# Relu's first weight as a second scalar operand, and a bias tile's load moved behind a store

## The chip, the cores and the metric

The kernel runs on one core of one Trainium2 chip. The metric is the device time of one execution in microseconds (us). Engines are named as in the profile: PE (matrix multiply), ACT (ScalarE), DVE (VectorE), POOL (GpSimd), and SP, whose queue issues almost all DMAs.

## The reference

Attention over 2 batches, 8 heads, 576 positions and head size 64, with a learned position bias, then a mixture of 4 experts over 1152 tokens, then a gated block in the same width of 512. What the change touches is the bias:

```python
psi_rel = np.log1p(np.abs(rel))                       # distance |i - j|
psi_i = np.log1p(np.maximum(pos[:, None], 1.0))
x = (psi_rel / psi_i)[..., None]
h = np.maximum(x @ w1 + b1, 0.0)                      # 32 hidden units
bias = h @ w2                                         # 8 heads
scores = scores + bias.transpose(2, 0, 1)[None]       # before the softmax
```

Since psi_i is positive, h is computed as max(w1 * log1p(distance) + b1 * psi_i, 0) / psi_i, and the division comes after the product with w2.

## The kernel before, in words

**Order of the work.** The kernel hands every operation to a planner (`Plan`) with an estimated time per engine, a priority, the buffers that it reads and writes, and operations that it comes `after`. The planner plays the work through in its own time and fixes one static order of instructions for each engine and for SP's queue. On the chip each engine keeps to its order and waits, by semaphores, for data and for buffers alone. An `after` shapes the order; it is no wait on the chip. All estimates stay as they are in what the change does not touch.

**The bias.** One DMA brings a table `cs` (line 337): the distances' logarithms (`tab`, 576 columns, the same in all 128 partitions), `neg_` (psi of the rows), `rinv` (1/psi), `cw` (w1 and b1, one column each) and `w2s`. Partitions are four groups of 32 hidden units. The bias rows come in 36 units `u` of 16 rows, each of four groups `g` (four rows each). `bias_group` makes a unit as follows. Each of four buffers `hh` takes one Relu over `n` columns (n is 576 for the first unit, 464 for the eighth, falls to 304 in the middle and rises again): three on DVE (line 376) and one on ACT (line 378), or all four on DVE in odd units among the first eight. DVE computes max(t, -b1 psi), which is the Relu less b1 psi; what is missing there is added later as a constant column `corr`, one of which (`corr[1]`) is zero for the group that ACT did. PE multiplies with `w2s` into PSUM (`pb`, line 390). The "side" copy (`put`, line 408 on ACT or 410 on DVE) scales by `rinv`, adds `corr` and writes a staging buffer `bst`; a "mirror" copy (line 239) fills the other side; a DMA stores the unit in DRAM, in `bias_d` (line 421). There are eight `hh` buffers and at first five `bst`.

**Who reads it.** Bias tiles `bt` of 128 rows are loaded from `bias_d` with shifted rows. The first tile, for the first eight units, is loaded in two halves of 64 rows (line 487): the first half needs units 0 to 3, the second units 4 to 7. The first attention groups then need `bt` in DVE's reduction (line 516), and all their later steps come behind it. Later tiles are loaded whole (line 476). The first 8 units have the highest rank (`bias0`), the next 8 `bias1`, the other 20 `bias2`; the latter are spread among the attention work until about 120 us. Expert matmuls (lines 772, 785), which PE uses to fill its time, start when the first attention groups are done, near 70 us.

**Ahead of the first Relu** stand, in the kernel before, a scaling of `tab` by w1 on ACT (line 345) and three scalings on DVE (`scales`, lines 340 to 342). `corr_mm` (line 353) and `corr_copy` (lines 357 and 359) make the constant column from b1 and w2.

Of the kernel before, what the change touches and what calls it, by code (L numbers as in the profile page):

```python
# [9 lines left out]
F32 = mybir.dt.float32  # L10
U32 = mybir.dt.uint32
F32R = mybir.dt.float32r
AF = mybir.ActivationFunctionType
ALU = mybir.AluOpType
# [3 lines left out]
B, H, S, D = 2, 8, 576, 64  # L18
HID = 32
P = 128  # L20
# [21 lines left out]
ENGINES = {"kcast": "ACT DVE", "ksub": "POOL DVE", "qcast": "DVE", "qsub": "DVE", "pt": "ACT DVE", "tail": "ACT DVE", "side": "ACT DVE", "mirror": "POOL ACT", "mirror0": "ACT DVE",  # L42
           "whi": "ACT DVE", "wlo": "DVE", "xhi": "DVE", "xlo": "POOL DVE", "rb": "ACT DVE", "rx": "ACT DVE", "s64": "DVE",
           "wsum": "POOL DVE", "whi2": "ACT", "wlo2": "DVE", "px": "ACT DVE", "xsum": "DVE", "xhi2": "ACT", "xlo2": "DVE", "hmul": "DVE", "hlo": "DVE"}
# [49 lines left out]
class Plan:  # L94
# [9 lines left out]
    def op(self, eng, fn, r=(), w=(), rw=(), hold=(), prio=0, lock=False, after=(), size=0, late=0):  # L104

        o = Op()
        o.eng, o.fn, o.prio, o.lock, o.size = eng, fn, prio, lock, size
        o.after, o.n, o.done, o.late = [], len(self.ops), False, late
        deps = set(after)
        for b in r:  # L110
            deps.update(b.writers)
        for b in rw:
            deps.update(b.writers)
            deps.update(b.readers)
        for b in rw:
            b.writers, b.readers = [o], []
        for b in w:
            b.writers.append(o)
        for b in r:
            b.readers.append(o)  # L120
        deps.discard(o)
        o.left = len(deps)
        for d in deps:
            d.after.append(o)
        o.bufs = list({id(b): b for b in (*r, *w, *rw, *hold)}.values())
        for b in o.bufs:
            b.left += 1
        self.ops.append(o)
        return o
# [102 lines left out]
def tile_kernel(ctx, tc, qd, kd, kf, vd, cst, probs, w1r, w2r, war, wbr, wor, out):  # L232
    nc = tc.nc
    plan = Plan()
    op = plan.op
# [14 lines left out]
    def t_psum(n, engs="ACT DVE"):  # L250
        est = {"ACT": n / 1.2 + 55, "DVE": n / 0.96 + 68}
        return {e: est[e] for e in engs.split()}
# [32 lines left out]
    hp = tp(hp_stack, "hp", side="right")  # L285
# [50 lines left out]
    rinv, cw, w2s = cs_t[:, S + NG:S + NG + NU], cs_t[:, S + NG + NU:S + NG + NU + 2], cs_t[:, S + NG + NU + 2:]  # L336
    op({"SP": 440}, lambda e: nc.sync.dma_start(out=cs_t, in_=cst), w=[cs], size=P * 3160)

    def scales(e):
        nc.vector.tensor_scalar(out=pos, in0=neg_.rearrange("p (u g) -> p u g", g=4)[:, :, 4 - pos.shape[2]:], scalar1=cw[:, 1:2], scalar2=None, op0=ALU.mult)  # L340
        nc.vector.tensor_scalar(out=neg_, in0=neg_, scalar1=cw[:, 1:2], scalar2=-1.0, op0=ALU.mult, op1=ALU.mult)
        nc.vector.tensor_scalar(out=w2s, in0=w2s, scalar1=8.0, scalar2=None, op0=ALU.mult)

    lg = Buf(t=cs_t)
    op({"ACT": S / 1.2 + 200}, lambda e: nc.scalar.activation(out=tab, in_=tab, func=AF.Copy, scale=cw[:, 0:1]), r=[cs], w=[lg], prio=-1)
    op({"DVE": 450}, scales, r=[cs], w=[lg])
    cs = lg
    pc, cr = new("tv", "pc"), Buf(t=cs_t)


    def corr_mm(e):
        for g in range(4):
            nc.tensor.matmul(pc.t[32 * g:32 * g + 32, 0:1], w2s, cw[:, 1:2], start=True, stop=True)

    def corr_copy(e):
        for n, x in corr.items():
            nc.vector.tensor_copy(x, pc.t[:, 0:1])
            for g in range(4 - n, 4):
                nc.vector.memset(x[32 * g:32 * g + 32], 0.0)

    def dist(u):
        before, after = 16 * u + 15, S - 16 * u
        return before, after, max(before + 1, after)

    rows, early = [], []

    def bias_group(u, rank):
        pri, acts = RANK[rank], RELUS[rank] if u % 2 == 0 or rank != "bias0" else 0
        before, after, n = dist(u)
        hs = []  # L370
        for g in range(4):
            G = 4 * u + g
            hh = new("hh")
            hs.append(hh)
            if g < 4 - acts:
                op({"DVE": n / 1.92 + 130}, lambda e, hh=hh, G=G: nc.vector.tensor_scalar(out=hh.t[:, :n], in0=tab[:, :n], scalar1=neg_[:, G:G + 1], scalar2=None, op0=ALU.max), r=[cs], w=[hh], prio=pri, lock=True)  # L376
            else:
                op({"ACT": n / 1.2 + 220}, lambda e, hh=hh, G=G: nc.scalar.activation(out=hh.t[:, :n], in_=tab[:, :n], func=AF.Relu, bias=pos[:, u, g - 4:][:, :1]), r=[cs], w=[hh], prio=pri)
        pb = new("tv" if n <= 512 else "s", "pb")
        bst = new("bst")  # L380


        def base():
            return (pb.t, 0) if n <= 512 else (pb.t.rearrange("p a b -> p (a b)"), 512 - n // 2)

        def mm(e):
            t, o = base()
            for lo, hi in ((0, n),) if n <= 512 else ((0, n // 2), (n // 2, n)):
                for g in range(4):
                    nc.tensor.matmul(t[32 * g:32 * g + 32, o + lo:o + hi], w2s, hs[g].t[:, lo:hi], start=True, stop=True)  # L390

        op({"PE": n * 1.67 + 170}, mm, r=[*hs, cs], w=[pb], hold=[bst], prio=pri)


        def ends():
            t, o = base()
            b = bst.t
            if before >= after:
                side = b[:, 0:before + 1], t[:, o:o + 1 + before][:, ::-1]
                rest = b[:, before + 1:before + after], b[:, before - after + 1:before][:, ::-1]  # L400
            else:
                side = b[:, before:before + after], t[:, o:o + after]
                rest = b[:, 0:before], b[:, before + 1:2 * before + 1][:, ::-1]
            return side, rest

        def put(e, out, src):
            if e == "ACT":
                nc.scalar.activation(out=out, in_=src, func=AF.Identity, scale=rinv[:, u:u + 1], bias=corr[acts])  # L408
            else:
                nc.vector.tensor_scalar(out=out, in0=src, scalar1=rinv[:, u:u + 1], scalar2=corr[acts], op0=ALU.mult, op1=ALU.add)  # L410

        def mirror(e):
            copy(e, *ends()[1])

        m = min(before, after - 1)
        side = op({e: v + 95 for e, v in t_psum(n, ENGINES["side"]).items()}, lambda e: put(e, *ends()[0]), r=[pb, cr], w=[bst], prio=pri)
        op({e: v for e, v in {"POOL": 2 * m + 150, "ACT": m / 1.2 + 95, "DVE": m / 0.96 + 68}.items() if e in ENGINES["mirror0" if rank == "bias0" else "mirror"].split()}, mirror, w=[bst], after=[side], prio=pri)
        rows.append(Buf(t=bias_d))

        def store(e):  # L420
            nc.sync.dma_start(out=bias_d[16 * u:16 * u + 16, :, S - before:S + after].rearrange("i h j -> (i h) j"), in_=bst.t[:, :before + after])

        o = op({"SP": 440}, store, r=[bst], w=[rows[u]], prio=pri, size=P * 4 * (before + after))
        if u == P // 16 - 1:
            early.append(o)

# [7 lines left out]
    def bias_rows(i0, n, h, nh):  # L436
        row = H * BW - 1
        o = i0 * H * BW + h * BW + S - i0
        x = bias_d.rearrange("i h j -> (i h j)")[o:o + n * row].rearrange("(i w) -> i w", w=row)
        return x[:, :nh * BW].rearrange("i (h j) -> i h j", h=nh)[:, :, :S]  # L440
# [25 lines left out]
    def bias_tile(m, t):  # L466
        for x in bias_seq[-3:]:
            if x[:2] == (m, t):
                return x[2]
        bt = new("bt")  # L470
        bias_seq.append((m, t, bt))

        def load(e):
            b = bt.t
            if t < 4:
                nc.sync.dma_start(out=b, in_=bias_rows(t * P, P, 2 * m, 2))
            else:
                nc.sync.dma_start(out=b[0:D, 0:1], in_=bias_rows(4 * P, D, 2 * m, 1))
                rest = bias_rows(4 * P, D, 2 * m + 1, 1)
                nc.sync.dma_start(out=b[D:P, 0:1, :S - D], in_=rest[:, :, D:])  # L480
                nc.sync.dma_start(out=b[D:P, 0:1, S - D:], in_=rest[:, :, :D])

        need = min(P * t + P, S) // 16
        if t == m == 0:
            for h in range(2):
                r = slice(D * h, D * h + D)
                op({"SP": 440}, lambda e, h=h, r=r: nc.sync.dma_start(out=bt.t[r], in_=bias_rows(D * h, D, 0, 2)), r=rows[4 * h:4 * h + 4], w=[bt], size=D * 8 * S)
        else:
            op({"SP": 440 if t < 4 else 1320}, load, r=rows[:need], w=[bt], size=P * 8 * S, late=1000 if t else 0)
        return bt  # L490
# [642 lines left out]
    for b in range(B):  # L1133
        QK[0, b, 0] = plain(0, b)
    op({"PE": 600}, corr_mm, r=[cs], w=[pc])
    op({"DVE": 400}, corr_copy, r=[pc], w=[cr])
    for u in range(NU):
        bias_group(u, "bias0" if u < P // 16 else "bias1" if u < 256 // 16 else "bias2")
    for g in groups:
# [225 lines left out]
```

## Time and profile before

| | |
|---|---|
| median of 3 runs | 791.68 us (790.96 to 793.36) |
| the profiled execution | 791.38 us |
| its span, first to last instruction | 789.6 us |
| PE busy in the span | 774.2 us (98%) |
| DVE busy in the span | 649.5 us (82%) |
| ACT busy in the span | 404.3 us (51%) |

Times of instructions are from the start of the span. A busy PE is an engine with a matmul under way, not one at its peak. Most executions of one program agree within 0.3%.

### The profile page before, as it was taken

The page shows a single profiled execution, that of the slowest core. Times are in us where ns is not written, and L with a number is a line of the kernel's source. Part 1 is how long each engine was busy: PE and PEld are TensorE (multiplying, and loading weights), DVE is VectorE, ACT ScalarE, POOL GpSimd, SP SyncE. Part 2 cuts the span into 40 slices and gives each one's busy share as a digit, 9 for nine tenths or more (in the row PEclk, how much of TensorE's full clock was granted, in tenths as well). Part 3 has the DMA queues.
Part 4 walks back from the last instruction along what each step waited for, and adds up shares of the span by engine and source line. Part 5 has one row for each costly group of instructions (what it writes and reads, how often), then busy time and mean ns, then how long its engine had stood idle before and what let it go on. Part 6 is the DMA issues. An engine that isn't in the chain of part 4 may idle for free.

```text
span 789.6 us, 13146 instructions
## 1 busy us (share of the span) xinstructions
PE 774.2 (98%) x4933; PEld 662.3 (84%) x4933; DVE 649.5 (82%) x1374; ACT 404.3 (51%) x848; POOL 28.1 (4%) x46
## 2 busy tenths in 40 slices
PE   7998999999999999999999999999999999999997
PEld 3475678888988888888888888889889999999996
DVE  7899986889896687998989998988698985757545
ACT  6877765677766543544544535344466532433321
POOL 0000100000000000000000000010010100000000
PEclk9999999999999999999999999999999999999999
DMA  6996658677563134455545653545405340301103
GB/s 233 327 344 215 232 178 276 218 243 244 179 208 98 45 96 127 134 166 175 160 126 159 204 175 120 166 132 161 134 1 183 112 160 1 107 27 55 54 1 120
DMA packets 46432, 120.31 MB, mean 152 GB/s; under 512 B 5024, under 2 KB 9376, under 8 KB 46368
## 3 DMA queue, kind: packets, MB, share of 16 engines
q1 hardware_dynamic: 46224, 119.34, 46.6%
q8 instruction: 39, 0.64, 0.3%
q14 instruction: 25, 0.20, 0.1%
q10 hardware_dynamic: 144, 0.13, 0.0%
HBM read 93.62 MB, written 25.84 MB: 151 GB/s over the span
## 4 chain that ended last, share of the span: by engine, by line
PE 90%; DVE 6%; ACT 1%; issue 1%; DMA 1%; DVEq 0%; ACTq 0%
PE pz L785 32%; PE up L883 14%; PE pw L1030 9%; PE up L772 8%; PE pb L390 4%; PE pv L613 4%; PE pr L1030 4%; PE ps L513 4%; PE pt L548 4%; PE pq L1030 2%; PE ps L531 1%; PE pz L1110 1%; DVE pr L516 1%; DVE k L453 1%; PE rp L593 1%
## 5 line engine op out<-in xcount | busy, mean ns | idle before, releaser
L785 PE MATMUL pz<-wh,hh 128*128 128x512 f32 x386 | 153.2, 397 | 0.0
L785 PE MATMUL pz<-wh,hl 128*128 128x512 f32 x386 | 151.3, 392 | 0.0
L785 PE MATMUL pz<-wl,hh 128*128 128x512 f32 x386 | 151.2, 392 | 0.0
L785 PEld LDWEIGHTS pz<-wl,hh 128*128 128x128 f32 x386 | 72.5, 188 | 15.9
L785 PEld LDWEIGHTS pz<-wh,hh 128*128 128x128 f32 x386 | 72.5, 188 | 14.2 <-issue 1.8
L785 PEld LDWEIGHTS pz<-wh,hl 128*128 128x128 f32 x386 | 72.5, 188 | 12.2
L239 ACT COPY ct<-pw 128x640 f32<-128x640 f32 (+3 forms) x48 | 27.9, 582 | 85.0 <-PE pw L1030 85.0
L516 DVE CUSTOM_DVE_ANT_0 pr<-ps,bt 128x576 f32<-128x576 f32 (+1 forms) x80 | 59.9, 753 | 13.9 <-PE ps L513 11.3
L658 DVE TENSOR_TENSOR wl<-wst,wh 128x1024 fp32r<-128x1024 f32 (+1 forms) x60 | 69.7, 1162 | 1.9 <-ACT wh L239 1.6
L526 ACT ACTIVATE pr<-pr,sums 128x576 f32<-128x576 f32 x72 | 56.1, 780 | 15.3 <-DVE sums L516 10.4
L772 PE MATMUL up<-x_h,wh 128*128 128x256 f32 (+1 forms) x200 | 61.7, 308 | 0.7 <-DVE hl L796 0.7
L239 ACT CAST wh<-wst 128x1024 fp32r<-128x1024 f32 (+1 forms) x56 | 54.5, 974 | 15.1 <-PE pz L785 7.8
L772 PE MATMUL up<-x_h,wl 128*128 128x256 f32 (+1 forms) x200 | 57.3, 286 | 0.0
L772 PE MATMUL up<-x_l,wh 128*128 128x256 f32 (+1 forms) x200 | 57.2, 286 | 0.0
L239 ACT COPY ptb<-pt 128x512 f32<-128x512 f32 (+3 forms) x98 | 40.3, 438 | 30.8 <-PE pt L548 25.4
L376 DVE TENSOR_SCALAR hh<-cs 128x560 f32<-128x560 f32 (+17 forms) x112 | 43.9, 448 | 3.8 <-PE pb L390 3.6
L239 ACT COPY ct<-up 128x448 f32<-128x448 f32 x39 | 20.7, 531 | 47.8 <-PE up L883 47.6
L613 PE MATMUL pv<-ptb,v 128*64 128x128 f32 (+2 forms) x480 | 44.1, 331 | 0.3 <-ACT bst L408 0.3
L883 PE MATMUL up<-xb,wsh 128*128 128x448 f32 x156 | 44.3, 365 | 0.0
L1125 DVE TENSOR_TENSOR acc<-pz,acc 128x512 f32<-128x512 f32 x44 | 30.2, 689 | 15.9 <-PE pz L785 14.9
L772 PEld LDWEIGHTS up<-x_h,wh 128*128 128x128 f32 x200 | 37.6, 188 | 6.5 <-issue 3.0
L548 PE MATMUL pt<-ident,pr 128*128 128x128 f32 x288 | 41.7, 275 | 0.0
(194 smaller groups left out, 1844.8 us busy)
## 6 DMA issues: line engine op xcount, KB each, us to landing
wst<-in_w1r SPq DMA_DIRECT2D x30, 512.0 KB, 4.4
wst<-in_w2r SPq DMA_DIRECT2D x30, 512.0 KB, 4.5
bias_d<-bst SPq DMA_DIRECT2D x36, 295.5 KB, 4.1
bt<-bias_d SPq DMA_DIRECT2D x15, 576.0 KB, 5.3
v<-in_vd SPq DMA_DIRECT2D x24, 320.0 KB, 4.3
s<-in_war SPq DMA_DIRECT2D x12, 512.0 KB, 4.9
wz_d<-hl SPq DMA_DIRECT2D x24, 256.0 KB, 2.5
s<-in_wbr SPq DMA_DIRECT2D x12, 512.0 KB, 4.9
```

The costliest lines, as they stand in the source:

```text
L239: (nc.scalar.copy if e == "ACT" else engine[e].tensor_copy)(out, in_)
L376: op({"DVE": n / 1.92 + 130}, lambda e, hh=hh, G=G: nc.vector.tensor_scalar(out=hh.t[:, :n], in0=tab[:, :n], scalar1=neg_[:, G:G + 1], sca ...
L390: nc.tensor.matmul(t[32 * g:32 * g + 32, o + lo:o + hi], w2s, hs[g].t[:, lo:hi], start=True, stop=True)
L516: nc.vector.tensor_tensor_reduce(out=pr.t[r0:r1, c].rearrange("p (a b) -> p a b", a=2), in0=ps.t[r0:r1, :, :HS], in1=bt.t[r0:r1, c].rearra ...
L526: nc.scalar.activation(out=pr.t[:, c], in_=pr.t[:, c], func=AF.Exp, scale=-1.0, bias=sums.t[:, neg:neg + 1], accum_out=sums.t[:, col:col + 1])
L548: nc.tensor.transpose(pt.t[:, kt * P:kt * P + P], pr.t[:, s, k0:k0 + P], ident)
L613: nc.tensor.matmul(pv.t[s * D:(s + 1) * D, :w], V.t[:, s, kt * D:(kt + 1) * D], ptb.t[:, blk, :w], start=(kt == 0), stop=(kt == 4))
L658: op(t_two(1024 - skip, ENGINES["wlo"]), lambda e: engine[e].tensor_tensor(out=w.t[1][:, skip:], in0=wst.t[:, skip:], in1=f(w.t[0][:, skip ...
L772: nc.tensor.matmul(u.t[:, :n], block(a, ft, d), x_at(x, d, lo, n), start=(d == 0 and j == 0), stop=(d == 3 and j == 2))
L785: nc.tensor.matmul(z.t, a[:, ft, tt * P:(tt + 1) * P], bb[:, ft, :], start=(first and ft == 0 and j == 0), stop=(final and ft == 1 and j = ...
L883: nc.tensor.matmul(bank.t[:, :n], s(a, k), x(b, k), start=(first and k == 0 and i == 0), stop=(stop and k == 1 and i == 2), skip_group_che ...
L1030: nc.tensor.matmul(o_, s[:, k], d[:, k], start=(first and k == 0 and i == 0), stop=(k == 1 and i == 2), skip_group_check=True)
```

## The change

The table `tab` is no longer scaled ahead of the Relus. DVE's Relu takes two operations with two scalars of one value per partition: it multiplies by w1 and takes the maximum with -b1 psi. ACT's Relu takes w1 as its `scale` operand, beside the `bias` operand that it had. Of the scalings, -b1 psi is made on DVE into a buffer of its own, b1 psi for ACT's groups on ACT, and the factor 8 goes from `w2s` to `rinv` (on DVE, with a lower rank) and to the constant column. POOL sets the `corr` columns to zero in advance, and `corr_copy` is two instructions in place of two copies and a memset. `corr_mm` needs only the table's DMA. The two half loads of the first bias tile come `after` the store of the seventh unit (u = 6) in the planner.

```diff
--- before.py
+++ after.py
@@ -336,15 +336,11 @@
     rinv, cw, w2s = cs_t[:, S + NG:S + NG + NU], cs_t[:, S + NG + NU:S + NG + NU + 2], cs_t[:, S + NG + NU + 2:]
     op({"SP": 440}, lambda e: nc.sync.dma_start(out=cs_t, in_=cst), w=[cs], size=P * 3160)
 
-    def scales(e):
-        nc.vector.tensor_scalar(out=pos, in0=neg_.rearrange("p (u g) -> p u g", g=4)[:, :, 4 - pos.shape[2]:], scalar1=cw[:, 1:2], scalar2=None, op0=ALU.mult)
-        nc.vector.tensor_scalar(out=neg_, in0=neg_, scalar1=cw[:, 1:2], scalar2=-1.0, op0=ALU.mult, op1=ALU.mult)
-        nc.vector.tensor_scalar(out=w2s, in0=w2s, scalar1=8.0, scalar2=None, op0=ALU.mult)
-
-    lg = Buf(t=cs_t)
-    op({"ACT": S / 1.2 + 200}, lambda e: nc.scalar.activation(out=tab, in_=tab, func=AF.Copy, scale=cw[:, 0:1]), r=[cs], w=[lg], prio=-1)
-    op({"DVE": 450}, scales, r=[cs], w=[lg])
-    cs = lg
+    psi, neg_ = neg_, hp.tile([P, NG], F32, name="neg")
+    NEG, POS, RI = Buf(t=neg_), Buf(t=pos), Buf(t=cs_t)
+    op({"DVE": 220}, lambda e: nc.vector.tensor_scalar(out=neg_, in0=psi, scalar1=cw[:, 1:2], scalar2=-1.0, op0=ALU.mult, op1=ALU.mult), r=[cs], w=[NEG], prio=-1)
+    op({"ACT": 220}, lambda e: nc.scalar.activation(out=pos, in_=psi.rearrange("p (u g) -> p u g", g=4)[:, :, 4 - pos.shape[2]:], func=AF.Copy, scale=cw[:, 1:2]), r=[cs], w=[POS], prio=-1)
+    op({"DVE": 90}, lambda e: nc.vector.tensor_scalar(out=rinv, in0=rinv, scalar1=8.0, scalar2=None, op0=ALU.mult), r=[cs], w=[RI], after=[], prio=0.1)
     pc, cr = new("tv", "pc"), Buf(t=cs_t)
 
 
@@ -352,17 +348,18 @@
         for g in range(4):
             nc.tensor.matmul(pc.t[32 * g:32 * g + 32, 0:1], w2s, cw[:, 1:2], start=True, stop=True)
 
+    for n, x in corr.items():
+        nc.gpsimd.memset(x, 0.0)
+
     def corr_copy(e):
         for n, x in corr.items():
-            nc.vector.tensor_copy(x, pc.t[:, 0:1])
-            for g in range(4 - n, 4):
-                nc.vector.memset(x[32 * g:32 * g + 32], 0.0)
+            nc.vector.tensor_scalar(out=x[:P - 32 * n], in0=pc.t[:P - 32 * n, 0:1], scalar1=8.0, scalar2=None, op0=ALU.mult)
 
     def dist(u):
         before, after = 16 * u + 15, S - 16 * u
         return before, after, max(before + 1, after)
 
-    rows, early = [], []
+    rows, early, sixth = [], [], []
 
     def bias_group(u, rank):
         pri, acts = RANK[rank], RELUS[rank] if u % 2 == 0 or rank != "bias0" else 0
@@ -373,9 +370,9 @@
             hh = new("hh")
             hs.append(hh)
             if g < 4 - acts:
-                op({"DVE": n / 1.92 + 130}, lambda e, hh=hh, G=G: nc.vector.tensor_scalar(out=hh.t[:, :n], in0=tab[:, :n], scalar1=neg_[:, G:G + 1], scalar2=None, op0=ALU.max), r=[cs], w=[hh], prio=pri, lock=True)
+                op({"DVE": n / 1.92 + 130}, lambda e, hh=hh, G=G: nc.vector.tensor_scalar(out=hh.t[:, :n], in0=tab[:, :n], scalar1=cw[:, 0:1], scalar2=neg_[:, G:G + 1], op0=ALU.mult, op1=ALU.max), r=[cs, NEG], w=[hh], prio=pri, lock=True)
             else:
-                op({"ACT": n / 1.2 + 220}, lambda e, hh=hh, G=G: nc.scalar.activation(out=hh.t[:, :n], in_=tab[:, :n], func=AF.Relu, bias=pos[:, u, g - 4:][:, :1]), r=[cs], w=[hh], prio=pri)
+                op({"ACT": n / 1.2 + 220}, lambda e, hh=hh, G=G: nc.scalar.activation(out=hh.t[:, :n], in_=tab[:, :n], func=AF.Relu, scale=cw[:, 0:1], bias=pos[:, u, g - 4:][:, :1]), r=[cs, POS], w=[hh], prio=pri)
         pb = new("tv" if n <= 512 else "s", "pb")
         bst = new("bst")
 
@@ -413,7 +410,7 @@
             copy(e, *ends()[1])
 
         m = min(before, after - 1)
-        side = op({e: v + 95 for e, v in t_psum(n, ENGINES["side"]).items()}, lambda e: put(e, *ends()[0]), r=[pb, cr], w=[bst], prio=pri)
+        side = op({e: v + 95 for e, v in t_psum(n, ENGINES["side"]).items()}, lambda e: put(e, *ends()[0]), r=[pb, cr, RI], w=[bst], prio=pri)
         op({e: v for e, v in {"POOL": 2 * m + 150, "ACT": m / 1.2 + 95, "DVE": m / 0.96 + 68}.items() if e in ENGINES["mirror0" if rank == "bias0" else "mirror"].split()}, mirror, w=[bst], after=[side], prio=pri)
         rows.append(Buf(t=bias_d))
 
@@ -423,6 +420,8 @@
         o = op({"SP": 440}, store, r=[bst], w=[rows[u]], prio=pri, size=P * 4 * (before + after))
         if u == P // 16 - 1:
             early.append(o)
+        if u == P // 16 - 2:
+            sixth.append(o)
 
 
 
@@ -484,7 +483,7 @@
         if t == m == 0:
             for h in range(2):
                 r = slice(D * h, D * h + D)
-                op({"SP": 440}, lambda e, h=h, r=r: nc.sync.dma_start(out=bt.t[r], in_=bias_rows(D * h, D, 0, 2)), r=rows[4 * h:4 * h + 4], w=[bt], size=D * 8 * S)
+                op({"SP": 440}, lambda e, h=h, r=r: nc.sync.dma_start(out=bt.t[r], in_=bias_rows(D * h, D, 0, 2)), r=rows[4 * h:4 * h + 4], w=[bt], size=D * 8 * S, after=sixth)
         else:
             op({"SP": 440 if t < 4 else 1320}, load, r=rows[:need], w=[bt], size=P * 8 * S, late=1000 if t else 0)
         return bt
@@ -1133,7 +1132,7 @@
     for b in range(B):
         QK[0, b, 0] = plain(0, b)
     op({"PE": 600}, corr_mm, r=[cs], w=[pc])
-    op({"DVE": 400}, corr_copy, r=[pc], w=[cr])
+    op({"DVE": 200}, corr_copy, r=[pc], w=[cr])
     for u in range(NU):
         bias_group(u, "bias0" if u < P // 16 else "bias1" if u < 256 // 16 else "bias2")
     for g in groups:
```

## Rows read from the trace of the kernel before

**Rows 1.** The page's first part: busy us (share of the span), instructions.

```profile
PE 774.2 (98%) x4933; PEld 662.3 (84%) x4933; DVE 649.5 (82%) x1374; ACT 404.3 (51%) x848; POOL 28.1 (4%) x46
```

**Rows 2.** Windows: stretch, length, busy us of PE, PEld, DVE, ACT, POOL.

```profile
52.81:70.00 17.19, 14.63 (x154) 11.05 (x154) 16.88 (x48) 14.04 (x32) 0.41 (x1) 1.00 0.72 248
70.00:130.00 60.00, 60.00 (x467) 42.39 (x468) 49.87 (x107) 41.91 (x79) 6.03 (x11) 1.00 0.65 219
```

**Rows 3.** Chain that ended last, first 75 us: start, us, what.

```profile
4.02 0.79 ACT cs L345
...
27.76 1.25 issue
...
53.52 0.36 DVE hh L376
```

**Rows 4.** Timeline of DVE from 3.9 us: start, us, what, count.

```profile
4.31 0.29 DVE L341 TENSOR_SCALAR cs<-cs 128x144 f32<-128x144 f32 x1
...
4.83 3.06 DVE L376 TENSOR_SCALAR hh<-cs 128x576 f32<-128x576 f32 x7
7.81 0.21 DVE L357 COPY corr<-pc 128x1 f32<-128x1 f32 x2
```

**Rows 5.** DVE's groups by shape, first 130 us: busy us, mean ns, idle before.

```profile
L239 DVE COPY ptb<-pt 128x512 f32<-128x512 f32 x9 | 6.2, 686 | 0.0
...
L376 DVE TENSOR_SCALAR hh<-cs 128x512 f32<-128x512 f32 x6 | 2.6, 480 | 0.2 <-PE pb L390 0.2
...
L937 DVE TENSOR_SCALAR acc<-pz,gate 128x512 f32<-128x512 f32 x2 | 1.5, 748 | 1.6 <-PE pz L785 1.6
...
L410 DVE TENSOR_SCALAR bst<-pb,cs,corr 128x528 f32<-128x528 f32 x1 | 0.8, 822 | 0.0
```

**Rows 6.** Timeline of DVE near 18 us, and from 22 to 29 us.

```profile
18.17 0.76 DVE L410 TENSOR_SCALAR bst<-pb,cs,corr 128x464 f32<-128x464 f32 x1 [0.27 <-ACT bst L408]
18.85 0.44 DVE L376 TENSOR_SCALAR hh<-cs 128x432 f32<-128x432 f32 x1
...
24.19 1.99 DVE L376 TENSOR_SCALAR hh<-cs 128x368 f32<-128x368 f32 x6 [1.12 <-PE pb L390]
28.15 0.76 DVE L516 CUSTOM_DVE_ANT_0 pr<-ps,bt 128x576 f32<-128x576 f32 x1 [1.96 <-DMA bt<-bias_d]
```

**Rows 7.** Timeline of SP's queue, 17 to 20 us; its waits, first 30 us.

```profile
18.51 0.71 SPq L487 DMA_DIRECT2D bt<-bias_d  x1
19.32 1.01 SPq L421 DMA_DIRECT2D bias_d<-bst  x2
...
SPq L487 <- DMA bias_d<-bst: 2.4, 3, 0.8
```

**Rows 8.** DMAs issued at 10 to 13, 19.9 and 24.2 us: KB, us to landing.

```profile
bias_d<-bst SPq DMA_DIRECT2D x3, 295.5 KB, 2.1
...
bias_d<-bst SPq DMA_DIRECT2D x1, 295.5 KB, 4.2
...
bt<-bias_d SPq DMA_DIRECT2D x1, 288.0 KB, 3.9
```

**Rows 9.** Timeline of ACT, 15 to 20 us: mirrors of units 6 and 7.

```profile
18.11 0.28 ACT L239 COPY bst<-bst 128x111 f32<-128x111 f32 x1
...
18.96 0.30 ACT L239 COPY bst<-bst 128x127 f32<-128x127 f32 x1
```

**Rows 10.** Windows of line 376 alone: stretch, length, DVE busy us (count).

```profile
4.02:18.00 13.98, 12.62 (x31) 1.00 0.67 260
18.00:28.15 10.15, 6.22 (x18) 1.00 0.78 244
28.15:52.81 24.66, 3.16 (x9) 1.00 1.02 372
52.81:70.00 17.19, 4.44 (x12) 1.00 0.72 248
70.00:130.00 60.00, 17.43 (x42) 1.00 0.65 219
```

## The prediction

> **What bounds the kernel now.** I read the page first, then the busy times by stretch, then the chain that ended last, then DVE's and SP's timelines around the edit. PE is busy nearly throughout [rows 1], so the end moves only by what PE idles or is held up. The stretches tell where that can be: from 52.8 to 70 us PE is busy 14.63 of 17.19 us and DVE 16.88, so there DVE sets the pace and PE idles 2.56 us; from 70 to 130 us PE is busy 60.00 of 60.00 us and DVE has 10 us to spare [rows 2]. The chain says the same: it begins on the scaling of the table, has 1.25 us of "issue" at 27.8 us, before PE's scores of the second group, and passes onto DVE (a Relu among others) from 53 us [rows 3]. The edit lies wholly ahead of 130 us. What it gains or loses must be carried through 28 to 70 us, where the work is a single line of attention groups, to reach the end; behind that PE has other work to fill with.
>
> One place in this prologue matters most. DVE's first reduction waits 1.96 us for the bias tile and starts at 28.15 us [rows 6]. The second half of that tile is issued at 24.2 us, once unit 7's store has landed, and takes 3.9 us [rows 8]. That store went out at 19.9 us and took 4.2 us, where the first three took 2.1 us [rows 8]. Ahead of it on SP stood the first half's load: SP waited up to 0.8 us at a time for earlier stores [rows 7], the load went out at 18.51 us and held the queue 0.71 us, and only then came the stores of units 6 and 7 [rows 7], though unit 6's mirror had been done at 18.11 + 0.28 = 18.39 us [rows 9].
>
> **The change part by part.**
>
> *Scalings ahead of the Relus.* The table's scaling on ACT takes 0.79 us from 4.02 us [rows 3], and the first Relu starts at 4.83 us [rows 4]. Afterwards a DVE Relu waits only for -b1 psi, an instruction like the one of 0.29 us in [rows 4], and ACT's for a smaller one. 4.02 + 0.29 and a few hundredths for the semaphore is 4.35: a gain of 0.48 us. The rescaled `rinv` runs while the Relu waits for its semaphore; if it comes in the way, the gain is 0.3. ACT's scale operand I cost at nothing, since the side copy and the table's scaling on ACT already carry one. POOL's memsets run before the table lands.
>
> *The second scalar.* No row shows a DVE instruction in SBUF with two per-partition scalars. The nearest read PSUM: 512 columns take 686 ns as a plain copy and 748 ns with one scalar; with two, 528 columns take 822 ns [rows 5] and 464 columns 0.76 us [rows 6], so about 0.95 ns a column and 807 ns for 512. Each scalar costs about 60 ns. I take 0.06 us more for every DVE Relu, 540 ns in place of 480 for 512 columns [rows 5]. Lower bound: nothing. Upper bound: that two scalars cost the Relu its double rate; it would then go like the PSUM row, 807 in place of 480 ns, 0.33 us more each. I choose 0.06 because the one-scalar Relu already runs at the double rate and the step from none to one is the same 60 ns. There are 112 DVE Relus: 31 until 18 us, 18 until 28.15, 9 until 52.8, 12 until 70 and 42 until 130 us [rows 10].
>
> [...]
>
> *The constant column.* Two copies, a memset and their wait hold DVE from 7.81 to about 8.18 us, where the seven Relus behind them begin; two instructions should take 0.1 us less.
>
> *Unit 7.* DVE's side copy of unit 7 stands at 18.17 us behind 31 Relus: 31 x 0.06 = 1.86 us later, less 0.48 and 0.10 from above, less its idle 0.27 [rows 6], less some 0.2 us idle earlier (13.98 us, of which Relus 12.62 [rows 10], scalings 0.81 and the constant 0.37): 0.8 us later. Its mirror then ends at 19.26 [rows 9] + 0.8 = 20.1 us, and the store goes out at about 20.1 instead of 19.9.
>
> *The load behind the seventh store.* Unit 6's store can now go at 18.4 instead of 19.32 us, and no load is in front of unit 7's. I give that store 2.6 us to land, between the 2.1 of the first three and the 4.2 of before: 22.7 instead of 24.1 us. The planner will let the loads go only when it thinks unit 6's store landed; by its formula that is 3.3 us after issue, so units 7 and 8 probably go first. The moved load costs its 0.71 us of SP then, right ahead of the second half, and shares the DMA engines with it; I add 0.4 us to the 3.9: landing at 27.1 instead of 28.15. Next late is DVE itself: its last Relus before the reduction end at 24.19 + 1.99 = 26.18 us [rows 6]; they come 49 x 0.06 = 2.9 us later, less 0.58, less the idle spells (0.27 + 0.2 + up to 1.12 [rows 6]), so 0.8 to 1.9 later, 27.0 to 28.1. I take 27.5: the first reduction gains **0.6 us** (bounds: 1.2 gained, 0.5 lost).
>
> *28 to 70 us.* The 12 Relus where DVE sets the pace cost 0.72 us in full; the 9 before, where PE mostly does, at most 0.54, taken as 0.2. **0.9 us lost** (0 to 1.3).
>
> *70 to 130 us.* 42 x 0.06 = 2.5 us on DVE, under its 10 us of room: **0**, and 2.5 if none of that room is where it is wanted. Behind 130 us no Relu is left.
>
> Sum: -0.6 + 0.9 = +0.3 us on the profiled 791.38, so 791.7. The median of the runs stands 0.3 above that execution; I say 791.8.
>
> About 0.3% (2.4 us) is what a measurement of this kernel can tell from no change.
>
> **The rivals.**
>
> *The second scalar is free.* Then the first reduction is set by the load at 27.1 us and nothing is given back: -1.0, 790.6 us. For it: the data rate need not change. Against it: [rows 5]. 0.12, within 0.3%. [...]
>
> *The load now comes too late.* If the planner puts unit 9's store ahead of the pair as well, the second half leaves up to 1 us later and lands behind 28.15: some 0.7 lost in place of 0.6 gained, about 793.1. Against it: before, the second half left at 24.2 behind the same stores. 0.10, still within 0.3%.
>
> *DVE no longer runs ahead of PE from 70 to 130 us (slower).* The orders are static and the planner's estimate of the Relu is unchanged, so it does not know of the 60 ns. If 2.1 of the 2.5 us reach PE, the sum passes 2.4 us; in full it is 0.3 + 2.5 = 2.8 us, 794.6. For it: 42 Relus lie there. Against it: DVE's room of 10 us, and PE without idle [rows 2]. 0.14. The half rate of the Relu is the far end of the same side: 112 x some 0.25 us, of which 10 us or more would show, above 801 us; 0.03.
>
> *The new order closes PE's gaps (faster).* All later operations are planned afresh from a start 0.5 us earlier. If the 1.25 us at 27.8 [rows 3] and most of the 2.56 us up to 70 us [rows 2] go, the kernel gains some 3.5 us: 788.3. For it: these are gaps of an order, not of a limit of PE. Against it: the second is DVE's own load, which grows. 0.17.
>
> **How the numbers follow.** The forecast has 0.44, so within 0.3% are 0.44 + 0.12 + 0.10 = 0.66, faster 0.17, slower 0.14 + 0.03 = 0.17. The range leaves out the better half of the closing gaps and the half rate, with some of the slow rival's top: 789.2 to 794.6.
>
> **What would show it.** The first Relu at 4.35 us; Relus of 512 columns at 540 ns; unit 6's store directly behind its mirror and both halves of the tile behind the stores of 7 and 8; the first reduction near 27.5 us with little wait for the DMA; DVE as full as before up to 70 us, and PE at 60 of 60 us behind it. Relus at 480 ns, a reduction behind 28.2 us, or PE idle between 70 and 130 us would each make a step wrong; a gain or a loss that sits behind 130 us would make the whole account wrong, since nothing in it reaches there.

## The result and the profile after

The changed kernel takes 796.92 us (median of six runs, 796.31 to 797.97). The kernel before, on the same chip, takes 792.71 us (790.96 to 794.94). The ratio is 1.0058, 95% interval 1.0044 to 1.0072: **slower by about 0.6%**, and outside the range of the prediction. The profiled execution after takes 796.31 us with a span of 794.5, so 4.9 us more than the one before; the rows below look for that difference.

The page's first part after, as in [rows 1]:

```profile
PE 777.7 (98%) x4933; PEld 661.6 (83%) x4933; DVE 656.1 (83%) x1381; ACT 403.3 (51%) x836; POOL 32.6 (4%) x51
```

For the same 4933 matmuls PE is busy 3.5 us longer and idle 1.4 us longer than before: most of the loss lies inside PE's busy time, and not in its gaps. POOL, which the prediction hardly speaks of, is busy 4.5 us longer; we come to it below. DVE's timeline after, as in [rows 4, 6]:

```profile
3.87 0.29 DVE L341 TENSOR_SCALAR neg<-cs 128x144 f32<-128x144 f32 x1 [3.87 <-DMA cs<-in_cst]
4.08 0.17 DVE L343 TENSOR_SCALAR cs<-cs 128x36 f32<-128x36 f32 x1
4.20 3.49 DVE L373 TENSOR_SCALAR hh<-cs,neg 128x576 f32<-128x576 f32 x7
7.60 0.21 DVE L356 TENSOR_SCALAR corr<-pc 128x1 f32<-128x1 f32 x2
7.74 1.49 DVE L373 TENSOR_SCALAR hh<-cs,neg 128x544 f32<-128x544 f32 x3
...
18.57 0.75 DVE L407 TENSOR_SCALAR bst<-pb,cs,corr 128x464 f32<-128x464 f32 x1
19.24 4.91 DVE L373 TENSOR_SCALAR hh<-cs,neg 128x432 f32<-128x432 f32 x12
24.73 2.35 DVE L373 TENSOR_SCALAR hh<-cs,neg 128x368 f32<-128x368 f32 x6 [0.58 <-PE pb L387]
29.42 0.76 DVE L515 CUSTOM_DVE_ANT_0 pr<-ps,bt 128x576 f32<-128x576 f32 x1 [2.34 <-DMA bt<-bias_d]
```

The first Relu starts 0.63 us earlier, but the first reduction starts at 29.42 us, 1.27 us later, and it waits 2.34 us for the bias tile, longer than before. The tile's second half is what it waits for. SP's queue shows why that load is late; as in [rows 7], first the timeline, then one of SP's waits in the first 40 us:

```profile
9.34 10.66 SPq L418 DMA_DIRECT2D bias_d<-bst  x8
20.17 0.71 SPq L486 DMA_DIRECT2D bt<-bias_d  x1
24.34 0.80 SPq L418 DMA_DIRECT2D bias_d<-bst  x2
25.31 0.61 SPq L486 DMA_DIRECT2D bt<-bias_d  x1
```

```profile
SPq L418 <- POOL bst L239: 3.7, 1, 3.7
```

The load's first half (20.17) stands behind unit 7's store, as the change wants it. Then come the stores of units 8 and 9, and only then the second half, at 25.31 us. Unit 8's store waits 3.7 us for POOL. It is a store that the second half does not need. POOL's only instruction of that time, after and before:

```profile
20.98 3.33 POOL L239 COPY bst<-bst 128x143 f32<-128x143 f32 x1 [19.60 <-ACT bst L405]
```

```profile
20.78 0.41 POOL L239 COPY bst<-bst 128x143 f32<-128x143 f32 x1 [19.48 <-ACT bst L408]
```

The same copy, unit 8's mirror, started at about the same time, takes 3.33 us in place of 0.41. It ends at 24.31 us, just behind DVE's unbroken run of twelve Relus (19.24 + 4.91 = 24.15). It looks as if POOL got nothing done while DVE ran those Relus; from here on the text calls that shut out.

The landings, as in [rows 8] (unit 7's store, and the second half; KB, us to landing), and the busy times while SP waited (PE, PEld, DVE, ACT, POOL, clock, DMA share, GB/s):

```profile
bias_d<-bst SPq DMA_DIRECT2D x1, 295.5 KB, 2.3
...
bt<-bias_d SPq DMA_DIRECT2D x1, 288.0 KB, 4.1
```

```profile
23.70:25.30 1.60, 1.60 (x19) 0.47 (x18) 1.02 (x4) 1.23 (x3) 0.89 (x2) 1.00 0.08 33
```

Unit 7's store, issued at 19.7 us with no load ahead of it, lands in 2.3 us (4.2 before). Its rows are there at 22.0 us, and the second half could have left then. It left 3.3 us later, and for 1.6 us of these the DMA engines had almost nothing to do (a share of 0.08).

Windows after, as in [rows 2], with one stretch more, and the chain's line that answers to the 1.25 us in [rows 3]:

```profile
52.81:70.00 17.19, 16.10 (x177) 12.49 (x172) 16.89 (x46) 13.52 (x27) 1.59 (x3) 1.00 0.72 244
70.00:130.00 60.00, 59.82 (x461) 40.57 (x461) 56.82 (x118) 44.13 (x85) 6.69 (x12) 1.00 0.70 233
130.00:200.00 70.00, 68.16 (x499) 60.16 (x499) 55.90 (x115) 44.06 (x103) 1.54 (x3) 1.00 0.69 225
```

```profile
28.51 1.78 issue
```

From 52.8 to 70 us PE is fuller than before. From 70 to 130 us it is still full, while DVE is busy 56.8 us in place of 49.9. From 130 to 200 us PE is busy 1.7 us less than the 69.85 us of before. From the 481st expert matmul (`up`, 291.94 us before, 296.98 after) to the last, the two kernels' matmuls come in one order, and each is 4.7 to 5.05 us late (4.9 at the last): the whole loss arises ahead of 292 us.

### The profile page after: what moved, and what is told of

Same layout as the page of the kernel before. It is cut to its first block, busy times and chain, and to the rows that moved or that the text cites. A ratio compares the mean times of both kernels' runs of the same rounds, so it can differ in the third digit from the quotient of the medians.

```text
span 794.5 us, 13138 instructions
## 1 busy us (share of the span) xinstructions
PE 777.7 (98%) x4933; PEld 661.6 (83%) x4933; DVE 656.1 (83%) x1381; ACT 403.3 (51%) x836; POOL 32.6 (4%) x51
## 4 chain that ended last, share of the span: by engine, by line
PE 81%; DVE 12%; DMA 3%; ACT 2%; issue 1%; POOL 0%; DVEq 0%; SPq 0%; ACTq 0%
PE pz L784 29%; PE up L882 14%; PE pw L1029 8%; PE up L771 6%; PE pv L612 5%; PE pr L1029 4%; PE ps L512 4%; PE pt L547 3%; PE pb L387 3%; PE pq L1029 2%; DVE hh L373 2%; DMA wst<-in_w1r 2%; DVE wl L657 1%; PE ps L530 1%; DVE pr L515 1%
## 5 line engine op out<-in xcount | busy, mean ns | idle before, releaser
L373 DVE TENSOR_SCALAR hh<-cs,neg 128x560 f32<-128x560 f32 (+17 forms) x112 | 50.3, 505 | 0.8 <-PE pb L387 0.6
L387 PE MATMUL pb<-hh,cs 128*32 128x288 f32 (+17 forms) x352 | 41.9, 502 | 1.8 <-DVE hh L373 1.8
```

## The experiments

All were timed in five rounds; times are medians, and ratios are against the kernel before on the same chip (791.58 to 791.68 us there, 792.71 beside the changed kernel). e1 to e4, e5 to e8 and e9 to e12 ran on three chips, so times from two groups, or with the changed kernel's, are compared by their ratios, or matmul by matmul in the profiles. There is one profile of each kernel. "First reduction" is the start of line 515's first instruction in the profile (28.15 us before, 29.42 after).

| kernel | us | ratio, 95% interval | first reduction | unit 8's mirror, us |
|---|---|---|---|---|
| e1_load_only | 793.43 | 1.0022 (1.0013 to 1.0032) | 27.62 | 0.41 |
| e2_relu_only | 796.74 | 1.0064 (1.0050 to 1.0077) | 29.45 | 3.33 |
| e3_one_scalar | 792.52 | 1.0012 (1.0003 to 1.0021) | 26.10 | 0.31 |
| e4_two_scalars_in_old | 795.63 | 1.0050 (1.0037 to 1.0062) | 30.02 | 3.42 |
| e5_mirror_on_act | 793.77 | 1.0027 (1.0016 to 1.0038) | 27.44 | on ACT, 0.30 |
| e6_load_before_stores | 794.91 | 1.0042 (1.0030 to 1.0054) | 27.21 | 3.33 |
| e7_one_pointer | 792.92 | 1.0018 (1.0009 to 1.0026) | 26.52 | 0.31 |
| e8_load_alone | 790.62 | 0.9991 (0.9982 to 1.0000) | 27.62 | 2.48 |
| e9_both_loads_first | 790.65 | 0.9986 (0.9977 to 0.9995) | 25.88 | 2.46 |
| e10_act_nudged | 796.41 | 1.0067 (1.0055 to 1.0080) | 29.66 | 3.24 |
| e11_scaled_behind | 789.96 | 0.9978 (0.9970 to 0.9987) | 25.83 | 2.45 |
| e12_no_act_scale | 793.59 | 1.0023 (1.0014 to 1.0032) | 26.27 | 0.41 |

**Which part of the change loses?** First each part alone (long lines of the diffs are shown by their changed end). e1 adds the planner's `after` to the kernel before:

```diff
+        if u == P // 16 - 2:
+            sixth.append(o)
...
-r=rows[4 * h:4 * h + 4], w=[bt], size=D * 8 * S)
+r=rows[4 * h:4 * h + 4], w=[bt], size=D * 8 * S, after=sixth)
```

> The kernel before with the loads of the first bias tile placed behind the seventh unit's store, and nothing else. If moving the load is what costs, it is slower by 3 to 5 us, with unit 8's and unit 9's stores ahead of the second half and the first reduction behind 29 us. If the second scalar's 60 ns on DVE cost, it is within 1.5 us of the kernel before, or faster by up to 1 us. If any new order of the planner's is slower by chance, it may be anywhere within 5 us.

e2 is the changed kernel without it:

```diff
-r=rows[4 * h:4 * h + 4], w=[bt], size=D * 8 * S, after=sixth)
+r=rows[4 * h:4 * h + 4], w=[bt], size=D * 8 * S)
```

> The changed kernel without the move of the loads. If the second scalar costs, it is slower than the kernel before by 3 to 6 us, as the changed kernel is. If the move of the loads costs, it is within 1 us of the kernel before.

e2 loses as much as the whole change, with the same stretched mirror. e1 loses a third as much, although its first reduction is 0.53 us earlier than before: a gain at the start that is gone by the end.

**The second scalar by itself, with the order of instructions kept.** e3 is the changed kernel with its order and with the old one-operation Relu on DVE (the product with w1 is left out):

```diff
-scalar1=cw[:, 0:1], scalar2=neg_[:, G:G + 1], op0=ALU.mult, op1=ALU.max)
+scalar1=neg_[:, G:G + 1], scalar2=None, op0=ALU.max)
```

> The changed kernel, its order of instructions the same on every engine, with DVE's Relus taking one scalar as before: the product with w1 is left out on DVE, so its time alone counts. If the second scalar costs, 512 columns go back to 480 ns, POOL's mirror of unit 8 from 3.3 us to about 0.4, and the time to the kernel before or some 1 to 2 us under it. If the new order costs, it stays 3 to 5 us above the kernel before.

e4 is the reverse, the kernel before with a second scalar that is 1.0:

```diff
+    one = hp.tile([P, 1], F32, name="one")
+    nc.gpsimd.memset(one, 1.0)
...
-scalar1=neg_[:, G:G + 1], scalar2=None, op0=ALU.max)
+scalar1=one, scalar2=neg_[:, G:G + 1], op0=ALU.mult, op1=ALU.max)
```

> The kernel before with a second scalar of 1.0 in each of DVE's Relus, everything else as it was (one more memset on POOL at the start). If the second scalar costs, it is slower by 3 to 6 us, with a long mirror copy on POOL somewhere among the Relus. If the new order costs, it is within 1 us of the kernel before.

Taking the second scalar out of the new order gives 3.6 us back by the ratios (1.0058 to 1.0012), and 3.9 at the last matmul of the profiles. Putting it into the old order costs 4.0 us (791.58 to 795.63), with everything else of the change absent. So the second scalar, with all that it sets off, is the main loss in both orders. e3's POOL, SP and DVE:

```profile
20.10 0.31 POOL L239 COPY bst<-bst 128x143 f32<-128x143 f32 x1 [18.72 <-ACT bst L405]
```

```profile
20.44 1.53 SPq L418 DMA_DIRECT2D bias_d<-bst  x2
22.13 0.61 SPq L486 DMA_DIRECT2D bt<-bias_d  x1
```

```profile
26.10 0.76 DVE L515 CUSTOM_DVE_ANT_0 pr<-ps,bt 128x576 f32<-128x576 f32 x1 [0.50 <-DMA bt<-bias_d]
```

The mirror is short, SP isn't held, the second half leaves at 22.13 us, and the first reduction comes 3.33 us earlier than after. As the two kernels keep one order, their matmuls can be compared one by one. The 3.3 us still stand at 54 us; the difference is 3.4 at 70 us, 4.3 at 111, 4.4 to 4.5 from 153 to 529, and 3.9 at the end. So three quarters of the 4.5 us arise ahead of the first reduction, and about 1.2 us later, nearly all of that behind 70 us.

**Is it the second operation or the second operand?** e7 keeps both operations and makes the first scalar an immediate, a constant in the instruction (the product with w1 is left out again):

```diff
-scalar1=cw[:, 0:1], scalar2=neg_[:, G:G + 1], op0=ALU.mult, op1=ALU.max)
+scalar1=1.0, scalar2=neg_[:, G:G + 1], op0=ALU.mult, op1=ALU.max)
```

> The changed kernel with the same order, DVE's Relu with both operations but the multiplication by a constant 1.0 in the instruction instead of w1 (the product with w1 is left out on DVE). If a second scalar operand costs and not a second operation, 512 columns take 480 to 490 ns, POOL's mirror about 0.4 us, and the time is that of the run with one scalar, some 4 us under the changed kernel. If the second operation costs, it is within 1 us of the changed kernel.

The group of 512 columns after, then in e7 (busy us, mean ns):

```profile
L373 DVE TENSOR_SCALAR hh<-cs,neg 128x512 f32<-128x512 f32 x6 | 3.0, 539 | 0.0
```

```profile
L373 DVE TENSOR_SCALAR hh<-cs,neg 128x512 f32<-128x512 f32 x6 | 2.6, 482 | 0.1
```

With one per-partition scalar the Relu takes 480 ns before, 482 with a second operation on an immediate, and 539 with a second per-partition scalar. The 60 ns belong to the operand, not to the operation.

**The hold-up, taken away in two ways.** e5 has ACT do unit 8's mirror; e6 leaves POOL's mirror and puts the stores of units 8 and 9 behind the second half's load:

```diff
         def mirror(e):
-            copy(e, *ends()[1])
+            copy("ACT" if u == 8 else e, *ends()[1])
```

> The changed kernel with the same order on every engine, but unit 8's mirror issued to ACT at its turn instead of POOL. If POOL's one mirror, held up by DVE's two-scalar Relus, is what delays the stores and the second half load behind it, the first reduction starts near 27.3 us instead of 29.42 and the kernel gains 1.5 to 2.2 us. If DVE's extra 60 ns alone set the loss, both stay within 0.5 us.

```diff
         def store(e):
+            if u in (8, 9) and not gone:
+                held.append(store)
+                return
...
+            def half_load(h, r):
+                nc.sync.dma_start(out=bt.t[r], in_=bias_rows(D * h, D, 0, 2))
+                if h:
+                    gone.append(1)
+                    for x in held:
+                        x("SP")
```

> The changed kernel with units 8's and 9's stores issued behind the second half load on SP instead of ahead of it; POOL's mirror stays where it is. If the loss comes through SP's queue, POOL's mirror is still over 3 us long but the first reduction starts near 27.3 us and the kernel gains 1.5 to 2.2 us. If POOL's mirror hurts in another way, nothing is gained.

SP and DVE in e5:

```profile
21.89 1.28 SPq L418 DMA_DIRECT2D bias_d<-bst  x2
23.34 0.61 SPq L486 DMA_DIRECT2D bt<-bias_d  x1
```

```profile
27.44 0.76 DVE L515 CUSTOM_DVE_ANT_0 pr<-ps,bt 128x576 f32<-128x576 f32 x1 [0.23 <-DMA bt<-bias_d]
```

SP, POOL and DVE in e6:

```profile
20.38 2.58 SPq L489 DMA_DIRECT2D bt<-bias_d  x2
24.55 0.81 SPq L422 DMA_DIRECT2D bias_d<-bst  x2
```

```profile
21.19 3.33 POOL L239 COPY bst<-bst 128x143 f32<-128x143 f32 x1 [19.80 <-ACT bst L406]
```

```profile
27.21 0.75 DVE L526 CUSTOM_DVE_ANT_0 pr<-ps,bt 128x576 f32<-128x576 f32 x1
```

Both bring the first reduction 2.0 to 2.2 us forward. e6 shows that the long mirror delays the first reduction only through the queue: it is still 3.33 us long, but the load no longer stands behind its store, and DVE waits for no DMA. Of the 3.3 us ahead of the first reduction, then, 2.0 to 2.2 are POOL's mirror and 1.1 to 1.3 DVE's own longer Relus (e5 and e6 stand 1.34 and 1.11 us behind e3 there). At the last matmul e5 is 2.5 us faster than the changed kernel and e6 1.4 (2.5 and 1.3 by the ratios). In e6 the stores of units 8 and 9 still leave late, at 24.55 us (21.89 in e5); whether that is why it ends behind e5 was not tried.

**Why is POOL shut out?** In e3 the mirror starts 2.03 us into DVE's run of Relus and takes 0.31 us, in the changed kernel 1.74 us into it; I supposed that it gets in when it starts late enough in the Relu that DVE has in hand, and let it start a little later with a one-column copy on ACT:

```diff
         def put(e, out, src):
+            if u == 8:
+                nc.scalar.copy(nudge, warm)
```

> The changed kernel with one added copy of one column on ACT ahead of unit 8's side copy, so that POOL's mirror starts about 0.2 us later against DVE's Relus. If POOL is shut out only when it starts in the first 0.12 us of a Relu in an unbroken run of them, the mirror takes 0.3 to 0.5 us, the first reduction starts near 27.5 us, and the kernel gains 1.5 to 3 us. If two-scalar Relus shut POOL out always, the mirror stays above 3 us and nothing is gained.

The mirror starts 0.07 us later and still takes 3.24 us. That start is 0.18 us into a Relu (0.09 in the changed kernel), so the 0.12 us of the expectation is not the limit with two scalars. The supposition itself is not refuted, for e10 moved the start too little. By the starts of the single Relus, unit 8's mirror got in with 0.06 to 0.16 us left until DVE's next Relu (before, e1, e3, e7, e12). It was shut out with 0.21 to 0.32 us left (after, e2, e6, e8, e9, e10, e11), and in e4, where it started together with a Relu. No run with two scalars had this mirror start in the stretch where one scalar let it in.

In the five profiles where the mirror begins inside the twelve two-scalar Relus (after, e2, e4, e6, e10) it is shut out each time, 3.24 to 3.42 us. With one scalar it is 0.31 to 0.41 us in five (before, e1, e3, e7, e12) and 2.45 to 2.48 in three (e8, e9, e11). So a shut-out is possible at one scalar too, and two scalars do not always bring it; a later copy on POOL in e4, and DVE's Relus around it:

```profile
82.04 0.50 POOL L239 COPY bst<-bst 128x207 f32<-128x207 f32 x1 [4.86 <-DMA bias_d<-bst]
```

```profile
81.43 2.25 DVE L378 TENSOR_SCALAR hh<-cs,one 128x416 f32<-128x416 f32 x5
```

This copy started among five two-scalar Relus, 0.20 us before the next, and was done 1.1 us before their end. Whether the second scalar shuts POOL out, or only moved the start of unit 8's mirror to a bad moment, stays open, and the time left is no general rule: in the kernel before, a copy at 79.51 us with 0.24 us left took 0.54 us and ended within its run of Relus. No run broke DVE's run to set POOL free: that the run is what holds POOL is read from the ends, which agree in all eight profiles, and not from an experiment.

**The load's move alone, without a new order.** e8 is the kernel before, its order kept, with the first half's load directly behind unit 7's store; e9 puts both halves there, ahead of units 8 and 9:

```diff
         def store(e):
+            dma(e)
+            if u == 7:
+                for x in held:
+                    x()
...
+                x = lambda: nc.sync.dma_start(out=bt.t[r], in_=bias_rows(D * h, D, 0, 2))
+                x() if h else held.append(x)
```

> The kernel before with its planned order on every engine, the first half load alone issued behind unit 7's store instead of ahead of unit 6's. If the move itself gains, the first reduction starts about 0.5 us or more before 28.15 and the kernel is 0.3 to 1.0 us faster. If the run with the move planned afresh was slower because of the move, this one is slower by 1 us or more.

```diff
         def store(e):
+            if u in (8, 9) and not gone:
+                held.append(dma)
+                return
+            dma(e)
+            if u == 7:
+                for x in first:
+                    x()
...
+                if not h:
+                    first.append(x)
+                    return
+                x()
+                gone.append(1)
+                for y in held:
+                    y("SP")
```

> The kernel before with its planned order on every engine, but both half loads of the first bias tile behind unit 7's store and ahead of units 8's and 9's. If the first reduction is carried through to the end when the order stays, it starts near 25.6 us (limited by DVE's last Relus, 26.18 less 0.5), and the kernel is 2 to 2.5 us faster than before. If what is gained there is lost later in any case, the kernel is within 0.5 us of before.

e8's POOL and SP, then e9's SP and DVE:

```profile
20.05 2.48 POOL L239 COPY bst<-bst 128x143 f32<-128x143 f32 x1 [18.74 <-ACT bst L408]
```

```profile
19.11 0.70 SPq L492 DMA_DIRECT2D bt<-bias_d  x1
22.55 0.81 SPq L427 DMA_DIRECT2D bias_d<-bst  x2
23.52 0.60 SPq L492 DMA_DIRECT2D bt<-bias_d  x1
```

```profile
19.55 3.08 SPq L496 DMA_DIRECT2D bt<-bias_d  x2
22.99 0.81 SPq L431 DMA_DIRECT2D bias_d<-bst  x2
```

```profile
25.88 0.76 DVE L536 CUSTOM_DVE_ANT_0 pr<-ps,bt 128x576 f32<-128x576 f32 x1
```

In e8 the shut-out appears with one scalar, and SP is held until 22.55 us. e9 passes it by: its first reduction is 2.27 us earlier than before. Of these 1.8 are left at 63.3 us and 0.5 to 0.6 from 66.8 us on; the time is 0.9986 of before. What was lost in between is not the order's. The windows of that stretch, in e9 and then in e11 (below), which has the same order of matmuls (PE, PEld, DVE, ACT, POOL, clock, DMA share, GB/s):

```profile
63.30:66.80 3.50, 3.50 (x18) 2.20 (x19) 3.37 (x10) 1.79 (x4) 0.40 (x1) 0.51 0.06 21
```

```profile
63.30:66.80 3.50, 3.50 (x32) 2.82 (x32) 3.37 (x10) 2.74 (x7) 0.42 (x1) 1.00 0.13 50
```

TensorE's granted clock was 0.51 there in e9's profiled execution and 1.00 in e11's, and PE ran 18 matmuls in place of 32. In the 3.3 us before, PE had been busy 1.61 us in e9 and 1.78 in e11, which lost nothing of its lead there.

e1 and e8 make the same move and have their first reduction at the same 27.62 us, but e1's later operations are planned afresh: it takes 793.43, e8 790.62 us (1.0022 and 0.9991), and at 292 us e1 stands 2.2 us behind the kernel before and e8 0.4 ahead of it. **A new plan by itself costs some 2.6 us here.** (e8's profiled execution took 792.65 us, 2.0 above its median: near 347 us it lost 1.4 us, with PE waiting 1.1 us for DVE once.)

**The ACT Relu's scale.** e12 is e3 without it:

```diff
-func=AF.Relu, scale=cw[:, 0:1], bias=pos[:, u, g - 4:][:, :1])
+func=AF.Relu, bias=pos[:, u, g - 4:][:, :1])
```

> The changed kernel in its order with one scalar on DVE and with no scale operand on ACT's Relus either; the product with w1 is left out on both. If ACT's scale operand costs nothing, the time is within 0.4 us of the run with one scalar on DVE. If its extra 0.09 us on each of ACT's Relus counts, it is 0.5 to 1.5 us faster than that run.

ACT's Relu of 512 columns after, and in e12:

```profile
L375 ACT ACTIVATE hh<-cs,pos 128x512 f32<-128x512 f32 x2 | 1.6, 810 | 0.0
```

```profile
L375 ACT ACTIVATE hh<-cs,pos 128x512 f32<-128x512 f32 x2 | 1.4, 712 | 0.0
```

The scale costs ACT 0.1 us a Relu and the kernel nothing that shows: e12's last matmul starts within 0.06 us of e3's. (Its ratio is 0.0011 higher than e3's without the scale; the intervals of the two overlap.)

**A version from these.** e11 keeps the order of before, has both half loads behind unit 7's store, and takes the second scalar only for units 0 and 1. Behind its first Relu, ACT scales the table into another buffer, and all later Relus take that and one scalar:

```diff
+            if u < 2:
+                nc.vector.tensor_scalar(out=hh.t[:, :n], in0=tab[:, :n], scalar1=cw[:, 0:1], scalar2=neg_[:, G:G + 1], op0=ALU.mult, op1=ALU.max)
+            else:
+                nc.vector.tensor_scalar(out=hh.t[:, :n], in0=tab2[:, :n], scalar1=neg_[:, G:G + 1], scalar2=None, op0=ALU.max)
...
+                nc.scalar.activation(out=tab2, in_=tab, func=AF.Copy, scale=cw[:, 0:1])
```

> The kernel before with its planned order, both half loads placed as in the run with both loads first, and the changed kernel's start: units 0 and 1 take w1 as a second scalar, ACT scales the table into another buffer behind its first Relu, and all later Relus read that with one scalar. If the start's 0.5 us is real and is carried when the order stays, the kernel is 2.5 to 3 us faster than before. If the start gains nothing behind PE's first units, it is as fast as the run with both loads first.

```profile
25.83 0.76 DVE L552 CUSTOM_DVE_ANT_0 pr<-ps,bt 128x576 f32<-128x576 f32 x1 [0.19 <-DMA bt<-bias_d]
```

Its first reduction is 2.3 us earlier than before, and 1.7 us are kept from 94 us on. That first reduction is e9's to within 0.05 us, so e11 shows no gain from the start with two scalars. At 789.96 us it is the fastest of all that ran, 0.9978 of before, though its interval overlaps e9's.

## Why the prediction was wrong

**Right.** The second scalar costs 0.06 us: 539 ns, forecast 540. The rival "The second scalar is free" does not hold here: 512 columns took 539 ns with two per-partition scalars and 480 with one. The half rate did not come either: from 304 to 576 columns the Relu went from 434 to 578 ns after and from 373 to 515 before, 0.53 and 0.52 ns a column. ACT's scale was put at nothing and costs 98 ns for 512 columns, but no time of the kernel that shows. The head's gain of 0.48 us came (the other 0.15 of the 0.63 is the table's DMA, which landed earlier). Unit 7's store landed sooner without a load ahead of it, in 2.3 us (forecast 2.6). The 0.4 us that the second half was given on top of its 3.9, for a load beside it, was an estimate; it took 4.1 us, issued 5.1 us behind the first half. DVE's side copy of unit 7 came 0.4 us late, half of what was forecast; the windows of the Relus alone, as in [rows 10], show 1.63 us more for the first 31 in place of 1.86, and the constant column gave back 0.2:

```profile
4.00:18.50 14.50, 14.25 (x31) 1.00 0.71 268
18.50:29.42 10.92, 7.41 (x19) 1.00 0.63 198
...
70.00:130.00 60.00, 22.60 (x48) 1.00 0.70 233
```

**Failed: "The load behind the seventh store".** The step forecast the first reduction at 27.5 us, from DVE's own lateness and from a second half that leaves once unit 7's store has landed. DVE's part was right: with the hold-up taken away, e5 and e6 have 27.44 and 27.21 us. But the step named the stores of units 7 and 8 ahead of the loads without asking what unit 8's store waits for. POOL's mirror was not priced at all. That is 1.9 us. How long the shut-out would last, no row of before could tell: there the same copy took 0.41 us.

**The rival "The load now comes too late"** had the right queue and sign, with unit 9's store as the cause and 0.7 us as the price. The cause was unit 8's store behind POOL, and the first reduction went 1.27 us past that of before.

**Failed: "70 to 130 us" at nothing.** The sum for the second scalar behind the first reduction, 0.9 us, came near by luck: against e3 it is 1.2 us in the changed kernel, 0 in e5, 1.5 in e6, and in the old order (e4, 1.9 us late at its first reduction and 3.5 from 170 us on) 1.6. But the text put all of it between 28 and 70 us. There e4 lost 0.8 us, as forecast, and the changed kernel 0.1; the rest, 0.9 and 1.1 us, came behind 70 us, most of it by 130. The text had read PE's 60 of 60 us and DVE's 10 us of room as safety. The rival "DVE no longer runs ahead of PE" came true in part. A full PE shows no gap, but its matmuls can still come later: of the changed kernel's 4.9 us, 3.5 are longer busy time.

**Failed: the new order as a gain only.** The text priced the planning afresh solely as a rival that closes PE's gaps. The gap before 70 us did shrink (PE 16.10 us in place of the 14.63 in [rows 2]). But e3, 2.05 us ahead at its first reduction, is 0.55 us behind the kernel before from 292 to 529 us: 2.6 us are lost behind the first reduction. The old order loses some of such a lead too (e11: 0.6 of 2.3), so about 2.2 us are the new order's: at 292 us e3 stands 2.2 us behind e11, and the changed kernel 1.5 behind e4, though its first reduction is 0.6 us earlier. e1 against e8 shows 2.6 with another new order. Part of it lies behind 130 us (from 130 to 200 us PE is busy 68.57 us in e3, 69.85 before), where the text said that nothing would reach. Which operations lose it I have not taken apart.

Together: forecast +0.3 us; add 1.9 for POOL, 0.3 for the later term and 2.6 for what e3 loses, and it is 5.1 us, where the profiles show 5.0 at 292 us and 4.9 at the end. The terms are read from the same profiles, so this is a tally and not a check.

## What to carry to other kernels

When a load is moved in a queue, ask of every transfer that now stands ahead of it which engine releases it, and price that engine's work too: here a copy on an almost idle POOL (busy 4% of the span) held a load that did not need it. Measure an edit with the order of instructions kept, and the planner's new order separately; a first reduction 2.3 us earlier was worth 1.7 us in the old order (e11), and one 2.05 us earlier ended in a loss in the new one (e3). Read the granted clock of a stretch before its loss is put down to an order (0.51 from 63.3 to 66.8 us in e9). The second per-partition scalar was not free here although it replaced a pass over the data: 0.06 us times 112 against one pass of 0.8 us.

## What the runs showed of the hardware

- A POOL copy of 128x143 between SBUF buffers, 0.31 to 0.41 us in five profiles, took 2.45 to 3.42 us in eight others, to the end of an unbroken run of twelve DVE Relus. It was so in all five profiles with two scalars and in three of eight with one; what decides stays open. DVE hardly paid where POOL got in: its twelve Relus lasted 4.23 us in e3, 4.19 in e8, where POOL was shut out.
- On DVE in SBUF a second per-partition scalar cost 57 to 59 ns for 512 columns (539 against 482 and 480), an immediate with its operation 2 ns; on ACT a `scale` operand beside a `bias` cost 98 ns for 512 columns (712 to 810 ns).
- Unit 7's store took 4.2 us to land with a load shortly ahead of it in SP's queue (3.3 and 3.5 in e2 and e4), 2.3 us in the changed kernel and 2.1 to 3.0 in the ten other runs without that load. The load is not the only thing that lengthens a store: in e12 one at 13.73 us, ahead of any such load, took 4.2 us.
